# Attention with a learned feature map plus a gated MLP: V weights in halves, and part of the MLP's elementwise work moved from VectorE to ScalarE and GpSimd

## The chip, the cores and the metric

One core of one Trainium2 chip. The metric is the device time of one execution in microseconds (us), as the median of several. Engines: PE is TensorE (matmuls; PEld its weight loads), DVE is VectorE, ACT is ScalarE, POOL is GpSimd, SP issues the DMAs. SBUF and PSUM are the two on-chip memories that this kernel uses; its matmuls write PSUM, which it divides into banks. Most executions of one kernel lie within 0.7% of each other (before: 281.5 to 283.3 us in its first six runs).

## The reference, cut to what matters

2048 tokens of width 640 are normalized. Two branches read the result, and both are added to the input.

```python
def _A_ref(x, wqkv, w_phi, wo):             # 32 heads of 20
    qkv = ...(x @ wqkv)...                  # q, k, v
    pq = einsum("bhsd,hdf->bhsf", q, w_phi) # the same for pk
    phi_q = concat([softmax(pq), softmax(-pq)])   # the same for phi_k
    kv  = einsum("bhsf,bhsd->bhfd", phi_k, v);  z = sum of phi_k over s
    num = phi_q @ kv;  den = phi_q @ z + 1e-6
    return (num / den).reshape(B, S, D) @ wo

def _B_ref(x, w1, w3, w2):                  # F = 1536
    return (silu(x @ w1) * (x @ w3)) @ w2

return x + _A_ref(layernorm(x), ...) + _B_ref(layernorm(x), ...)
```

## The kernel before

The kernel orders its own instructions. The body yields units of work (a K tile, an MLP unit, an attention tile and so on) in eight streams. At each step a greedy scheduler asks a small cost model which unit could start on PE first, and emits that one. The order on every engine is therefore fixed when the kernel is built, from modelled times.

```python
def tt(eng, o, a, b, f, fast=1):            # a two-input elementwise operation
    c = 0.16 + free(o) / 960 / fast if eng == "DVE" else 0.2 + free(o) * 1.7 / 1000
    P.op(eng, "tensor_tensor", [o], [a, b], (o, a, b, f), cost=c)
...
best = None                                 # the scheduler, for each stream's next unit
    at = max(P.ready(ops), P.free["PE"] + 0.15)
    if i == MLPS and P.free["DVE"] > P.free["PE"] + LAG:    # LAG = 4.0
        rank = n                            # an MLP unit comes last while DVE lags
    if best is None or (round(at, 2), rank) < best[:2]: best = ...
```

An MLP unit is 10 matmuls of 512 columns into two PSUM banks, one tanh on ACT, and two DVE instructions.

```python
act(th[:, n, :], bank(k), ACT.Tanh, 0.5)
stt(t1[:, n, :], th[:, n, :], 1.0, bank(k), ALU.add, ALU.mult)
stt(hT[b][:, fc, :], t1[:, n, :], 0.5, bank(k + 1), ALU.mult, ALU.mult)
```

An attention tile (128 tokens) is 12 small matmuls into four PSUM banks. ACT copies the denominators out, DVE combines them, multiplies them into the four banks (`prod`) and adds two halves. `pr`, `den` and `g` are tiny, and **each reads two tensors that lie in SBUF**. The next tile's matmuls reuse the four banks, so they wait for `prod`.

```python
# ... matmuls into four banks, seen as ps[:, n, head, 22]; columns 20 and 21 are denominators
for sg in range(2):
    act(e[:, sg:4 - sg:3 - 2 * sg, :]..., ps[:, 2 * sg:2 * sg + 2, :, 20:22], ACT.Copy)
tt("DVE", pr, e[:, 0:2, :], e[:, 2:4, :], ALU.mult)
tt("DVE", den, pr[:, 0, :], pr[:, 1, :], ALU.add)
P.op("DVE", "reciprocal", [den], [den], (den, den), cost=0.42)
tt("DVE", g, e[:, 2:4, :], den.unsqueeze(1).to_broadcast([128, 2, 32]), ALU.mult)
tt("DVE", p2..., ps[:, :, :, 0:DH], g.unsqueeze(3)..., ALU.mult)        # prod: PSUM x SBUF
tt("DVE", o_tok[:, t % 3, :], p2[:, 0, :], p2[:, 1, :], ALU.add, 2)
```

The start loads the tokens and V's weights, and normalizes four tiles; V and K tiles are projections. Before the first K tile, PE multiplies the feature map's weights into K's weights; this is called the fold here. Up to about 90 us tokens are normalized and V and K tiles are made (the token stage); the attention tiles follow (the attention stage).

```python
load_x(0, 1); load_x(1, 2); load_x(2, 4)
P.dma("SP", wv[:], wqkv_t[:, :, 2 * D:3 * D])
...
for t in range(4):                          # on DVE, in this order
    yield lambda t=t: ln_stats(t, 1)
    if t:
        yield lambda t=t: ln_apply(t - 1)
...
def proj(t, w, k):                          # a V or K tile
    for i in range(DC):
        for q in range(2):
            mm(bank(k + q, 320), xnT[:, i, ...], w[:, i, 320 * q:320 * q + 320], ...)
```

The softmax here doesn't subtract the row's maximum and nothing guards it: scores larger than these inputs give would overflow.

## Time and profile before

| | before |
|---|---|
| median of six runs | 282.28 us |
| profiled span | 280.7 us |
| PE busy | 274.5 us (98%) |
| DVE, ACT, POOL busy | 182.7, 106.9, 59.1 us |
| all matmuls but the last, each at the usual time from start to start of its width | 271.4 us (1889 matmuls, 639,648 columns) |
| first to last matmul start | 276.7 us |

The last two rows are worked out from the starts of the matmuls in the trace. The usual time is the mean of the intervals within 10% of the median: 215.8 ns for 512 columns, 135.8 for 320, 67.0 for 154, 38.4 for 88. The difference of the rows, 5.2 us, is all that PE lost.

The head of the page of before, then rows of its picture of the span in 40 slices. A digit is the busy share of one slice of 7.0 us in tenths.

```profile
PE 274.5 (98%) x1890; PEld 168.4 (60%) x1890; DVE 182.7 (65%) x320; ACT 106.9 (38%) x191; POOL 59.1 (21%) x90
...
PE   7899999999999999999999999999999999999996
...
DVE  5469969999564689989989997886663212121212
...
POOL 4417466999951000000000000000000000000000
```

PE is full (digit 9) from the third slice to the last but one. POOL is busy while K tiles are made (up to slice 12) and **idle in the attention stage**, where DVE is nearly full: from 92 to 190 us POOL is busy 0.43 us and DVE 86.6 of 98. The chain of work that ended last, followed back from the last instruction, by engine:

```profile
PE 94%; DMA 4%; SPq 2%; issue 0%; DVE 0%
```

Groups of instructions of before: engine, operation, output<-inputs, shapes, count | busy us, mean ns of one | idle before it.

```profile
L101 POOL TENSOR_TENSOR ekt<-ekt,rS_62 128x640 bf16<-128x640 bf16 x32 | 39.5, 1271 | 2.3 <-DVE rS_62 L101 2.3
...
L101 DVE TENSOR_TENSOR o_tok<-prod 128x640 bf16<-128x640 bf16 x16 | 7.9, 492 | 0.5
...
L101 DVE TENSOR_TENSOR pr_s<-e_s 128x64 f32<-128x64 f32 x16 | 3.6, 225 | 0.9 <-ACT e_s L101 0.4
L101 DVE TENSOR_TENSOR g_s<-e_s,den_s 128x64 f32<-128x64 f32 x16 | 3.6, 225 | 0.6
...
L101 DVE TENSOR_TENSOR den_s<-pr_s 128x32 f32<-128x32 f32 x16 | 3.1, 191 | 0.6
```

### The profile page before, as it was taken

What the parts mean: (1) busy time and instruction counts of PE and PEld (TensorE: products, weight loads), DVE (VectorE), ACT (ScalarE), POOL (GpSimd) and SP (SyncE); (2) the same over time, 40 slices, a digit from 0 to 9 for tenths busy, and PEclk for the clock granted to TensorE, in tenths of its full rate; (3) what the DMA queues carried; (4) which work ended last, traced back from release to release, by engine and by line L of the source; (5) the groups of instructions that cost most, each with busy time, mean ns of one, the idle gap of its engine ahead of it and who ended that gap; (6) DMA issues with size and microseconds to landing.
All of it is one profiled execution on the core that took longest, in us unless ns stands there. A gap on an engine that the chain in (4) does not pass through costs nothing.

```text
span 280.7 us, 4627 instructions
## 1 busy us (share of the span) xinstructions
PE 274.5 (98%) x1890; PEld 168.4 (60%) x1890; DVE 182.7 (65%) x320; ACT 106.9 (38%) x191; POOL 59.1 (21%) x90
## 2 busy tenths in 40 slices
PE   7899999999999999999999999999999999999996
PEld 2665765775469655555555565744446777777774
DVE  5469969999564689989989997886663212121212
ACT  3379969888520354464464522132221000000000
POOL 4417466999951000000000000000000000000000
PEclk9999999999999999999999999999999999999999
DMA  6973899630000672211111321230000131222211
GB/s 205 282 219 62 235 267 218 92 116 2 0 0 2 206 147 44 29 25 23 26 33 37 26 47 48 60 83 1 2 0 0 50 92 56 86 66 76 71 49 47
DMA packets 39654, 21.96 MB, mean 78 GB/s; under 512 B 26704, under 2 KB 39632, under 8 KB 39632
## 3 DMA queue, kind: packets, MB, share of 16 engines
q1 hardware_dynamic: 39632, 21.66, 32.0%
q8 instruction: 15, 0.25, 0.4%
q14 instruction: 7, 0.06, 0.1%
HBM read 12.81 MB, written 2.62 MB: 55 GB/s over the span
## 4 chain that ended last, share of the span: by engine, by line
PE 94%; DMA 4%; SPq 2%; issue 0%; DVE 0%
PE PS L101 94%; DMA wqkT<-in_A_wqkv_dram 4%; SPq L113 2%; DVE xres L101 0%
## 5 line engine op out<-in xcount | busy, mean ns | idle before, releaser
L101 PE MATMUL PS<-xnT,w_s 128*128 128x512 bf16 x480 | 106.7, 379 | 0.0
L101 PEld LDWEIGHTS PS<-xnT,w_s 128*128 128x128 bf16 x480 | 46.8, 98 | 55.5
L101 ACT ACTIVATE th<-PS 128x512 f32<-128x512 f32 x48 | 28.7, 597 | 57.9 <-PE PS L101 57.9
L101 DVE TENSOR_TENSOR xres<-PS,xres 128x640 bf16<-128x640 f32 (+2 forms) x17 | 13.4, 785 | 54.0 <-PE PS L101 54.0
L101 DVE SCALAR_TENSOR_TENSOR t_68<-th,PS 128x512 bf16<-128x512 f32 x48 | 32.8, 683 | 17.2 <-ACT th L101 17.2
L101 POOL TENSOR_TENSOR ekt<-ekt,rS_62 128x640 bf16<-128x640 bf16 x32 | 39.5, 1271 | 2.3 <-DVE rS_62 L101 2.3
L101 PE MATMUL PS<-wv,xnT 128*128 128x320 bf16 x160 | 24.2, 299 | 0.9 <-DMA wv<-in_A_wqkv_dram 0.9
L101 PE MATMUL PS<-wo_s,oT 128*128 128x320 bf16 (+2 forms) x160 | 24.5, 299 | 0.0
L101 DVE TENSOR_TENSOR prod<-PS,g_s 128x1280 bf16<-128x1280 f32 x16 | 23.9, 1491 | 0.6
L101 PE MATMUL PS<-Wkp,xnT 128*128 128x320 bf16 x160 | 23.9, 299 | 0.1
L101 PE MATMUL PS<-xnT,Wqp 128*128 128x512 bf16 x100 | 23.7, 379 | 0.0
L101 DVE TENSOR_REDUCE S_61<-ekt 128x64 f32<-128x1280 bf16 x16 | 23.0, 1438 | 0.0
L101 ACT ACTIVATE ekt<-PS 128x640 bf16<-128x640 f32 x32 | 20.7, 699 | 5.3 <-PE PS L101 5.0
L101 PEld LDWEIGHTS PS<-wv,xnT 128*128 128x128 bf16 x160 | 15.5, 98 | 6.9 <-ACT xnT L101 1.1
L101 PEld LDWEIGHTS PS<-wo_s,oT 128*128 128x128 bf16 x160 | 15.6, 98 | 6.1
L101 PEld LDWEIGHTS PS<-Wkp,xnT 128*128 128x128 bf16 x160 | 15.3, 98 | 6.3 <-ACT ekt L101 0.2
L101 DVE BATCH_NORM_STATS2 bst<-x_tok 128x6 f32<-128x320 bf16 x32 | 15.2, 476 | 5.4 <-DMA x_tok<-in_A_x_dram 4.9
L101 ACT ACTIVATE e_s<-PS 128x64 f32<-128x64 f32 x32 | 9.0, 282 | 21.9 <-PE PS L101 20.9
L101 PEld LDWEIGHTS PS<-xnT,Wqp 128*128 128x128 bf16 x100 | 9.4, 98 | 8.8
L101 PE MATMUL PS<-w_s,hT_79 128*128 128x320 bf16 (+2 forms) x96 | 13.9, 299 | 0.0
L101 PE MATMUL PS<-w_s,hT_71 128*128 128x320 bf16 x96 | 13.7, 299 | 0.0
L101 PE MATMUL PS<-w_s,hT_76 128*128 128x320 bf16 x96 | 13.7, 299 | 0.0
(59 smaller groups left out, 265.7 us busy)
## 6 DMA issues: line engine op xcount, KB each, us to landing
w_s<-in_B_w_dram SPq DMA_DIRECT2D x6, 640.0 KB, 7.4
xres<-in_A_x_dram SPq DMA_DIRECT2D x16, 160.0 KB, 2.4
out_dram<-xres SPq DMA_DIRECT2D x15, 160.0 KB, 1.8
x_tok<-in_A_x_dram SPq DMA_DIRECT2D x3, 640.0 KB, 5.8
w_s<-in_B_w_dram SPq DMA_DIRECT2D x1, 1920.0 KB, 9.4
wv<-in_A_wqkv_dram SPq DMA_DIRECT2D x1, 800.0 KB, 6.4
wo_s<-in_A_wo_dram SPq DMA_DIRECT2D x1, 800.0 KB, 4.7
x_tok<-in_A_x_dram SPq DMA_DIRECT2D x2, 160.0 KB, 2.3
```

The costliest lines, as they stand in the source:

```text
L101: o = _Op(eng, lambda: m(*args, **kw), r, w, cost)
L113: o = _Op(eng, lambda: m(out, in_), self.regions(in_), self.regions(out), nbytes, True)
```

## The change

Its intent: start V earlier, and take work off DVE, which lags in the attention stage, by giving ACT and POOL a share of it. When the model finds DVE late, ACT copies the second MLP bank from PSUM to SBUF (`up`), and POOL instead of DVE makes the product `hT`. POOL may also add the attention halves. To pay for `up` in SBUF, the tanh buffers go from three to two.

```diff
-        load_x(2, 4)
-        P.dma("SP", wv[:], wqkv_t[:, :, 2 * D:3 * D])
+        load_x(2, 3)
+        for a in (0, 320):
+            P.dma("SP", wv[:, :, a:a + 320], wqkv_t[:, :, 2 * D + a:2 * D + a + 320])
+        load_x(3, 4)
...
     def proj(t, w, k):
-        for i in range(DC):
-            for q in range(2):
+        for q in range(2):
+            for i in range(DC):
...
-        tt("DVE", o_tok[:, t % 3, :], p2[:, 0, :], p2[:, 1, :], ALU.add, 2)
+        eng = "POOL" if P.free["POOL"] < P.free["DVE"] else "DVE"
+        tt(eng, o_tok[:, t % 3, :], p2[:, 0, :], p2[:, 1, :], ALU.add, 2)
...
-        act(th[:, n, :], bank(k), ACT.Tanh, 0.5)
-        stt(t1[:, n, :], th[:, n, :], 1.0, bank(k), ALU.add, ALU.mult)
-        stt(hT[b][:, fc, :], t1[:, n, :], 0.5, bank(k + 1), ALU.mult, ALU.mult)
+        act(th[:, m, :], bank(k), ACT.Tanh, 0.5)
+        half = max(P.free["DVE"], P.free["ACT"] + 0.6, P.free["PE"] + 1.8) + 0.7
+        if max(half, P.free["ACT"] + 1.2, P.free["POOL"]) + 1.1 < half + 0.7 + 0.5 * (P.free["DVE"] - P.free["PE"]):
+            act(up[:, m, :], bank(k + 1), ACT.Copy, 0.5)
+            stt(t1[:, n, :], th[:, m, :], 1.0, bank(k), ALU.add, ALU.mult)
+            tt("POOL", hT[b][:, fc, :], t1[:, n, :], up[:, m, :], ALU.mult)
+        else:
+            ...                            # as before
```

Cut: the declarations of `up` and of two tanh buffers, and the model's DMA rate (320 to 305 thousand bytes per us).

More of the change, by code (lines that the diff above doesn't have):

```diff
@@ L178, in commit @@
                     self.free[o.eng] = t + max(1.3, o.cost / 150e3)
-                self.bus = max(self.bus, t + 0.5) + o.cost / (280e3 if o.part else 320e3)
+                self.bus = max(self.bus, t + 0.5) + o.cost / (280e3 if o.part else 305e3)
                 o.end = self.bus + 1.6
@@ L255, in bass_parallel_sum__linear_kernel_hedgehog__glu_gated_swiglu__prompt_kernel @@
     bf = DT.bfloat16
+    LAG = 4.0
     f32 = DT.float32
@@ L293, in bass_parallel_sum__linear_kernel_hedgehog__glu_gated_swiglu__prompt_kernel @@
     Wqp = new("Wqp", [128, DC, D], bf)
-    th = new("th", [128, 3, 512], f32)
+    th = new("th", [128, 2, 512], f32)
     t1 = new("t1", [128, 3, 512], bf)
+    up = new("up", [128, 2, 512], bf)
     xres = new("xres", [128, 4, D], bf)
@@ L573, in q_tok @@
            g.unsqueeze(3).to_broadcast([128, 4, 16, DH]), ALU.mult)
-        tt("DVE", o_tok[:, t % 3, :], p2[:, 0, :], p2[:, 1, :], ALU.add, 2)
+        eng = "POOL" if P.free["POOL"] < P.free["DVE"] else "DVE"
+        tt(eng, o_tok[:, t % 3, :], p2[:, 0, :], p2[:, 1, :], ALU.add, 2)
     nmlp = [0]
     def mlp(b, fc, k):
-        n = nmlp[0] % 3
+        n, m = nmlp[0] % 3, nmlp[0] % 2
         nmlp[0] += 1
@@ L585, in mlp @@
                    i == 0, i == DC - 1)
-        act(th[:, n, :], bank(k), ACT.Tanh, 0.5)
-        stt(t1[:, n, :], th[:, n, :], 1.0, bank(k), ALU.add, ALU.mult)
-        stt(hT[b][:, fc, :], t1[:, n, :], 0.5, bank(k + 1), ALU.mult, ALU.mult)
+        act(th[:, m, :], bank(k), ACT.Tanh, 0.5)
[5 more added lines that the diff above has]
+        else:
+            stt(t1[:, n, :], th[:, m, :], 1.0, bank(k), ALU.add, ALU.mult)
+            stt(hT[b][:, fc, :], t1[:, n, :], 0.5, bank(k + 1), ALU.mult, ALU.mult)
     finish = []
@@ L757, in outs @@
             yield lambda t=t: out_tile(t, banks(2))
-    MLPS, LAG = 6, 4.0
+    MLPS = 6
     URGENT = {0: 4.0, 3: 4.0}
```

## The prediction

Cuts in the text below are marked. One is a formula for the time of a matmul that is not taken from these traces, with the 271.2 us that it gave for all of them; the 5.4 us that the text goes on with is the 276.7 us less that. (From the trace's own intervals it is 5.2 us, in the table above.) The next is a term of 2.8 us for the first, slow matmuls, where the trace has 1.6 us. "At best about 2.5 us" was the estimate, near 5.4 less 2.8. The forecast's sum came to -0.4 to +0.5 us, centre +0.1, from the four numbered steps.

> **What bounds the kernel now.** TensorE. The page gives PE busy 274.5 us of a 280.7 us span (98%), DVE 65%, ACT 38%, POOL 21%; the chain that ended last is 94% PE and 4% one DMA (the transposing load of the K weights, 5.47 to 15.40 us).[...] first to last start took 276.7. Of the 5.4 us between, 4.8 lie before 16 us (timeline): [...]holes of 0.8 (first transpose), 0.3, 1.1 (V weights, landed 8.63) and 0.8 (K weights, landed 15.40). Later only about 0.7 us is lost, near 17, 47.4 and 48.1 us. At best the change can win about 2.5 us; 2% is 5.7 us.
>
> **What the change does.**
> 1. V weights in halves ahead of tile 3. V's first matmul waited until 8.77 us; the transposes of tiles 0 and 1 were done at 7.83. The first half should land near 6.2 (estimate: 410 KB at the old load's 278 GB/s), so V starts near 7.8: 0.9 gained. But tile 3 lands at 8.6 to 9.1 instead of 5.68, and DVE, in order, runs its statistics (1.0 us) before it normalizes tile 2, whose transpose goes from 10.12 to 10.4-10.7: the 0.9 is given back as a new hole. V ends near 15.4 instead of 14.8, about when the K weights land (15.4 to 15.8[...]). The fold starts at 15.6 to 15.9 instead of 15.54. Net 0 to 0.4 us lost.
> 2. V and K by column half: same matmuls and weight loads, 0 us in steady state. The first K tile needs all five folded chunks by its fifth matmul instead of its ninth (last eviction ended 18.29, K began 17.26): up to 0.5 us of hole, unless an MLP unit is put there, which I expect.
> 3. MLP up over ACT and POOL: DVE loses 0.687 us a unit, ACT gains 0.59, POOL about 1.05 (estimate from 1.271 us for a 640-element product). I guess 10 to 25 of 48 units. No PE wait of size after 17 us ends on DVE: 0 us.
> 4. Attention adds on POOL: DVE loses up to 16 x 0.492 = 7.9 us, POOL gains 16 x about 1.27 = 20. POOL is idle from about 90 us on. Latency grows 0.8 us, with tens of us of output work behind it: 0 us.
>
> Sum: -0.4 to +0.5 us, centre +0.1. PE has the same columns to pass and was not starved in the middle.
>
> **Predicted:** 282.9 us, 8 in 10 between 281.2 and 284.5 (the runs before spread 1.8 us). Faster by over 2%: 0.01; within 2%: 0.96; slower: 0.03.
>
> **What would show it.** Right: PE busy within 1 us of 274.5; DVE busy down 12 to 25 us, POOL up 30 to 45, span nearly unmoved; first V matmul near 7.8, then a wait of 0.5 to 1.3 us for normalized tile 2; fold at 15.5 to 16. Wrong: fold or first K over 0.5 us earlier, or PE holes over 0.3 us after 20 us.
>
> **What would make it wrong.** The static order comes from modelled times, so every engine's order can shift; a POOL product slowed by DVE beside it, or two tanh buffers instead of three, could hold PSUM banks and stall PE in the token stage. Or the MLP order fills the early holes: up to 1.5 us won.

## More of the kernel before

The model knows one duration for each instruction and the waits between instructions. It knows nothing of two engines hindering each other.

(The trace has 1.6 us for the first, slow matmuls: eight intervals of 0.39 to 0.43 us for 512 columns, at a granted clock of 1.00. Why they are slow is not shown.)

One attention tile in the timeline of before: start us, duration us, engine and so on. Lines of ACT, PEld and the DMA are left out.

```profile
118.20 0.85 PE L101 MATMUL PS<-KVc,EqT_81 128*128 128x154 bf16 x12
...
119.40 0.23 DVE L101 TENSOR_TENSOR pr_s<-e_s 128x64 f32<-128x64 f32 x1
119.66 0.19 DVE L101 TENSOR_TENSOR den_s<-pr_s 128x32 f32<-128x32 f32 x1
...
120.27 0.23 DVE L101 TENSOR_TENSOR g_s<-e_s,den_s 128x64 f32<-128x64 f32 x1
120.53 1.49 DVE L101 TENSOR_TENSOR prod<-PS,g_s 128x1280 bf16<-128x1280 f32 x1
```

From the first small matmul to the end of `prod` takes 3.8 us. The next tile's matmuls may then begin, but PE has other work meanwhile: in this order two MLP units (4.3 us) and a Q projection stand between most attention tiles.

## The result, and the profile after

The changed kernel takes 293.15 us (median of six, 292.17 to 293.65) against 282.28 us. The ratio is 1.038, with a 95% interval of 1.035 to 1.041. Ratios here and below are the mean time of one kernel's fast runs over that of the other's of the same rounds, so not quite the ratio of the medians. The prediction, 282.9 us with a range to 284.5, was wrong by 10 us.

The head of the page of the changed kernel, and the same rows of its slices (7.3 us each):

```profile
PE 275.9 (95%) x1872; PEld 167.4 (58%) x1890; DVE 175.2 (60%) x289; ACT 123.0 (42%) x221; POOL 98.3 (34%) x124
...
PE   7899989999999997988988999999999999999996
...
DVE  5378879996554699999999996445432121121212
...
POOL 4416868999932222222222534322310000000000
```

PE does the same work in 95% of a longer span: slices 16 to 22 now have gaps. POOL is busy in the attention stage. DVE gave up 31 instructions (320 to 289) yet saved only 7.5 us of busy time. (18 of the 1890 matmul records are missing from this trace.) The chain that ended last:

```profile
PE 73%; DVE 18%; DMA 3%; ACT 2%; SPq 2%; issue 1%
PE PS L101 73%; DVE prod L101 7%; DVE pr_s L101 5%; DVE den_s L101 3%; DMA wqkT<-in_A_wqkv_dram 3%; SPq L113 2%; DVE t_68 L101 1%; ACT e_s L101 1%; DVE g_s L101 1%; ACT up L101 1%; DVE o_tok L101 1%; ACT v_83 L101 0%; DVE xres L101 0%
```

DVE went from 0% to 18% of that chain, by way of the attention tile's own operations. The groups that answer to those of before, and POOL's new work:

```profile
L101 DVE TENSOR_TENSOR pr_s<-e_s 128x64 f32<-128x64 f32 x16 | 16.0, 1002 | 2.8 <-ACT e_s L101 1.4
...
L101 POOL TENSOR_TENSOR hT_78<-t_68,up 128x512 bf16<-128x512 bf16 x12 | 13.8, 1152 | 40.5 <-DVE t_68 L101 29.5 <-ACT e_s L101 11.0
...
L101 DVE TENSOR_TENSOR den_s<-pr_s 128x32 f32<-128x32 f32 x16 | 5.6, 352 | 0.6
L101 DVE TENSOR_TENSOR g_s<-e_s,den_s 128x64 f32<-128x64 f32 x16 | 3.6, 225 | 0.6
...
L101 POOL TENSOR_TENSOR o_tok<-prod 128x640 bf16<-128x640 bf16 x1 | 1.4, 1392 | 5.1 <-DVE prod L101 5.1
```

`pr_s`, the same 64 elements per partition, takes 1002 ns instead of 225, and `den_s` 352 instead of 191. Together that is 16.0 + 5.6 - 3.6 - 3.1 = 14.9 us more. `g_s` is unchanged. One tile in the timeline shows why:

```profile
128.96 0.86 PE L101 MATMUL PS<-KVc,EqT_82 128*128 128x154 bf16 x12 [0.73 <-DVE prod L101]
...
130.10 1.15 POOL L101 TENSOR_TENSOR hT_78<-t_68,up 128x512 bf16<-128x512 bf16 x1 [3.68 <-DVE t_68 L101]
130.17 1.16 DVE L101 TENSOR_TENSOR pr_s<-e_s 128x64 f32<-128x64 f32 x1
...
131.37 0.19 DVE L101 TENSOR_TENSOR den_s<-pr_s 128x32 f32<-128x32 f32 x1
...
131.98 0.23 DVE L101 TENSOR_TENSOR g_s<-e_s,den_s 128x64 f32<-128x64 f32 x1
...
132.24 1.49 DVE L101 TENSOR_TENSOR prod<-PS,g_s 128x1280 bf16<-128x1280 f32 x1
...
133.79 0.86 PE L101 MATMUL PS<-KVc,EqT_76 128*128 128x154 bf16 x12 [0.73 <-DVE prod L101]
```

POOL's product runs from 130.10 to 131.25. `pr_s` starts at 130.17 and ends at 131.33, just behind it. The same sight recurs: of the 48 executions of `pr_s`, `den_s` and `g_s`, 18 are long. Each of these 18 has a POOL product beside it and ends 0.05 to 0.08 us after that product. The 30 others take their usual time.

The loop closes over PSUM. From one tile's small matmuls to the next is 133.79 - 128.96 = 4.83 us. PE has only 3.93 us of work in it (0.69 for the 12 attention matmuls, 1.08 for a Q projection, 2.16 for an MLP unit, all at the usual times from start to start), so it waits 0.90 us for `prod`. (The timeline prints 0.73 us of idle time, because the modelled end of the matmul before it reaches into the gap.) Such holes between 103 and 175 us sum to 9.5 us, nearly the whole 9.7 us by which the profiled span grew. (In that sum gaps of 0.216 us are left out: they are the missing matmul records, all of 512 columns. The trace of the path alone, below, has all 1890 and shows the same holes, 9.5 us from 100 us on.)

The start behaved in part as predicted. V began at 7.67 instead of 8.77 us, and PE then lost 0.80 us at 8.9 us to normalized tile 2. The first half of V's weights landed at 6.30 us (predicted 6.2) and the second at 7.70. But tile 3 landed at 8.17 us, where I had predicted 8.6 to 9.1, and the fold began at 15.12 instead of the predicted 15.6 to 15.9. Differences of this size are not safe to read from one trace: V's weights in one piece (800 KB), with the very same loads before them in the queue, landed anywhere from 7.50 to 9.01 us in six traces (before, b1, b3, b4, c1 and e1; in order of size 7.50, 8.12, 8.17, 8.43, 8.63 and 9.01), and V began between 7.92 and 9.14 us.

### The profile page after: what moved, and what is told of

Same layout as the page of the kernel before. It is cut to its first block, busy times and chain, and to the rows that moved or that the text cites. A ratio compares the mean times of both kernels' runs of the same rounds, so it can differ in the third digit from the quotient of the medians.

```text
span 290.5 us, 4679 instructions
## 1 busy us (share of the span) xinstructions
PE 275.9 (95%) x1872; PEld 167.4 (58%) x1890; DVE 175.2 (60%) x289; ACT 123.0 (42%) x221; POOL 98.3 (34%) x124
## 4 chain that ended last, share of the span: by engine, by line
PE 73%; DVE 18%; DMA 3%; ACT 2%; SPq 2%; issue 1%
PE PS L101 73%; DVE prod L101 7%; DVE pr_s L101 5%; DVE den_s L101 3%; DMA wqkT<-in_A_wqkv_dram 3%; SPq L113 2%; DVE t_68 L101 1%; ACT e_s L101 1%; DVE g_s L101 1%; ACT up L101 1%; DVE o_tok L101 1%; ACT v_83 L101 0%; DVE xres L101 0%
## 5 line engine op out<-in xcount | busy, mean ns | idle before, releaser
L101 POOL TENSOR_TENSOR hT_78<-t_68,up 128x512 bf16<-128x512 bf16 x12 | 13.8, 1152 | 40.5 <-DVE t_68 L101 29.5
L101 ACT ACTIVATE up<-PS 128x512 bf16<-128x512 f32 x33 | 19.7, 598 | 15.4 <-PE PS L101 15.4
L101 DVE TENSOR_TENSOR prod<-PS,g_s 128x1280 bf16<-128x1280 f32 x16 | 23.9, 1491 | 0.5
L101 PE MATMUL PS<-xnT,Wqp 128*128 128x512 bf16 x93 | 22.2, 379 | 0.4
L101 PEld LDWEIGHTS PS<-Wkp,xnT 128*128 128x128 bf16 x160 | 15.4, 98 | 7.2 <-ACT ekt L101 1.1
L101 DVE TENSOR_TENSOR pr_s<-e_s 128x64 f32<-128x64 f32 x16 | 16.0, 1002 | 2.8 <-ACT e_s L101 1.4
L101 POOL TENSOR_TENSOR hT_72<-t_68,up 128x512 bf16<-128x512 bf16 x9 | 10.2, 1152 | 16.3 <-DVE t_68 L101 10.3
```

Source lines behind the costliest of these rows:

```text
L101: o = _Op(eng, lambda: m(*args, **kw), r, w, cost)
```

## The experiments

Theory S: a DVE operation with two SBUF inputs is held until the POOL instruction beside it ends. Theory O: the new order alone starves PE, because one MLP unit instead of two stands between attention tiles. Theory A: ACT's extra copies and the two tanh buffers hold PSUM banks.

| run | edit | median us | before, same rounds | ratio (95%) |
|---|---|---|---|---|
| a1_one_sbuf_input | after, `pr`, `den`, `g` with one SBUF input | 283.66 | 282.62 | 1.004 (1.000 to 1.008) |
| a2_no_mlp_path | after without the MLP path (two tanh buffers and the choice of engine for the add stay) | 294.63 | 282.62 | 1.043 (1.038 to 1.047) |
| b1_mlp_path_only | before with the MLP path | 292.79 | 282.62 | 1.037 (1.033 to 1.042) |
| b2_start_only | before with the early part | 291.32 | 282.62 | 1.031 (1.026 to 1.036) |
| b3_pool_two_input | before + unused POOL products | 293.00 | 281.88 | 1.037 (1.030 to 1.043) |
| b4_pool_one_input | before + unused POOL copies | 289.21 | 281.88 | 1.023 (1.017 to 1.029) |
| b5_start_lag5 | b2 with the lag limit 5 us | 285.51 | 281.88 | 1.010 (1.004 to 1.016) |
| c1_path_one_sbuf | b1 with a1's edit | 282.87 | 281.88 | 1.001 (0.996 to 1.007) |
| e1_fold_later | before, an MLP unit ahead of the fold | 282.49 | 282.40 | 1.002 (0.999 to 1.005) |
| e6_order_only | e1, V weights ahead of tile 3 | 283.46 | 282.40 | 1.004 (1.001 to 1.007) |
| e7_path_order | e6 + MLP path + a1's edit | 283.51 | 282.40 | 1.005 (1.001 to 1.008) |
| e2_all_fixed | after, all three mended | 282.97 | 282.40 | 1.003 (1.000 to 1.005) |

All outputs are right. Three or five rounds were run of each, so a run has four or six executions, and those of "before" are of the same rounds. b4's interval reaches from below to above 1.02, but all of it lies well above 1.

### The same order, without the second SBUF input

```diff
-        tt("DVE", pr, e[:, 0:2, :], e[:, 2:4, :], ALU.mult)
-        tt("DVE", den, pr[:, 0, :], pr[:, 1, :], ALU.add)
-        P.op("DVE", "reciprocal", [den], [den], (den, den), cost=0.42)
-        tt("DVE", g, e[:, 2:4, :], den.unsqueeze(1).to_broadcast([128, 2, 32]), ALU.mult)
+        tt("DVE", pr..., ps[:, :, :, 20], e[:, 2:4, :]..., ALU.mult)        # PSUM x SBUF
+        P.op("DVE", "tensor_reduce", [den], [pv], (den, pv, AX.X, ALU.add), ...)  # one input
+        dps = PS[:, k * 512 + 352:k * 512 + 384]       # unused columns of the tile's own bank
+        o = P.op("DVE", "reciprocal", [dps], [den], (dps, den), cost=0.42)
+        P.op("DVE", "tensor_tensor", [g], ..., (g, e[:, 2:4, :], db, ALU.mult), ...)  # db: dps; SBUF x PSUM
```

The kernel's own bookkeeping does not see a DVE write to PSUM that DVE reads next. An explicit dependency mended it. Modelled costs were kept, and the built program has the same order of instructions as the changed kernel on PE, ACT, POOL and DVE; only these operations differ. The POOL products, the ACT copies and the two tanh buffers all stay.

> The changed kernel with an unchanged order of instructions on all engines; only DVE's small attention ops (pr_s, den_s, g_s) no longer read two SBUF tensors: each reads one SBUF and one PSUM tensor, or one tensor. Theory S (a DVE op with two SBUF inputs is held until the POOL product beside it ends): pr_s falls from 1.00 us mean to under 0.3, the PE holes between 100 and 175 us go, and the time falls from about 293 to 283-286 us. Theory O (the new order alone, with an MLP unit between nearly all attention tiles, starves PE) and theory A (the added ACT copies and only two tanh buffers hold PSUM banks): 291-294 us.

Measured: 283.66 us, 9.5 us below the changed kernel (1.004 of before in its rounds, against 1.038). Two groups, and a tile of its timeline:

```profile
L102 DVE TENSOR_TENSOR pr_s<-PS,e_s 128x64 f32<-128x64 f32 x16 | 3.6, 224 | 5.6 <-ACT e_s L102 4.3
...
L102 POOL TENSOR_TENSOR hT<-t,up 128x512 bf16<-128x512 bf16 x33 | 37.9, 1153 | 73.2 <-ACT up L102 36.6 <-DVE t L102 36.6
```

```profile
122.41 1.15 POOL L102 TENSOR_TENSOR hT<-t,up 128x512 bf16<-128x512 bf16 x1 [2.97 <-DVE t L102]
122.48 0.23 DVE L102 TENSOR_TENSOR pr_s<-PS,e_s 128x64 f32<-128x64 f32 x1
122.74 0.22 DVE L102 TENSOR_REDUCE den_s<-pr_s 128x32 f32<-128x64 f32 x1
```

The same POOL product of 1.15 us runs beside `pr_s`, which now takes 0.23 us. In the stretch from 93 to 176 us PE is busy 83.0 of 83.0 us, against 75.5 in the changed kernel (76.1 in b1 below, whose trace lacks no matmul record). It is the second SBUF input that counts, and not SBUF as such: `den_s`, now a reduction of one SBUF tensor, lay beside a POOL product in 15 of its 16 executions and took 0.22 us in all of them. Theories O and A fall: with their order, copies and buffers in place the loss is gone. Consecutive attention tiles with one MLP unit between them now follow each other in 3.93 us (`pr_s` at 118.55 and 122.48 us), exactly PE's own work.

### A POOL instruction added to the kernel before

```diff
         stt(hT[b][:, fc, :], t1[:, n, :], 0.5, bank(k + 1), ALU.mult, ALU.mult)
+        if done["kv"]:                     # 39 of the 48 units; nobody reads `spare`
+            a = t1[:, n, 0:448].unsqueeze(1).to_broadcast([128, 2, 448])
+            P.op("POOL", "tensor_tensor", [o], [t1[:, n, :]], (o, a, a, ALU.mult), cost=0.01)
```

`o` is a view of `spare`, which takes unused bytes. The second run has two `tensor_copy` of the same 896 elements instead of the product. In both the order on PE, ACT and DVE is that of before.

> The kernel before with its order of instructions unchanged on PE, ACT and DVE; after each MLP unit of the attention stage POOL multiplies an 896-element bf16 tile with itself into a scratch tile that nobody reads (about 1.9 us, an estimate from 1.152 us for 512). Nothing else is changed, so nothing of order, tanh buffers or ACT copies. Theory S: pr_s beside it is held, to 1 us or more in most of 16 tiles, PE waits for prod, and the time rises by 4 to 14 us. Any theory that needs the new order or the ACT copies: 282 to 283.5 us and pr_s at 0.23.

> As the run before, but POOL makes two copies of 896 elements (one input each) instead of one product. If every POOL instruction holds DVE's ops with two SBUF inputs: pr_s near 1 us again and 4 to 14 us lost. If only POOL's two-input products hold them: pr_s at 0.23 us and 282 to 283.5 us.

Measured: 293.00 and 289.21 us. The groups of the run with products, then those of the run with copies:

```profile
L101 DVE TENSOR_TENSOR pr_s<-e_s 128x64 f32<-128x64 f32 x16 | 22.2, 1386 | 0.1
...
L101 POOL TENSOR_TENSOR spare<-t 128x896 bf16<-128x896 bf16 x39 | 65.6, 1681 | 67.4 <-DVE t L101 65.2
```

```profile
L101 DVE TENSOR_TENSOR den_s<-pr_s 128x32 f32<-128x32 f32 x16 | 12.9, 804 | 0.5
...
L101 DVE TENSOR_TENSOR g_s<-e_s,den_s 128x64 f32<-128x64 f32 x16 | 7.4, 461 | 0.6
...
L101 POOL COPY spare<-t 128x896 bf16<-128x896 bf16 x78 | 72.6, 931 | 56.4 <-DVE t L101 50.9
```

So POOL work that nobody needs, with no new order, no ACT copies and three tanh buffers, costs 11 us as products and 7 us as copies. The longer instruction holds longer: `pr_s` beside a 1.68 us product takes up to 1.71 us. A one-input copy of 0.93 us holds as well. There `pr_s` mostly slips in between two copies (263 ns in the mean) and `den_s` and `g_s` are caught instead. My alternative, that only products hold, is wrong. (`prod`, which reads PSUM and SBUF, took 1491 ns in every run, but in no trace did it run beside a POOL instruction, so it tests nothing. What does is `t`, which also reads PSUM and SBUF: in the changed kernel 14 of its 48 executions began inside a POOL product, and took 0.69 us, where the others took 0.63 to 0.69.)

### One part of the change at a time

> The kernel before with the ACT and POOL path of the MLP alone. All theories that blame the path: 291 to 294 us, with pr_s near 1 us. Under 286 would say that the path hurts only together with the other parts.

Measured: 292.79 us, with `pr_s` at 1.0 us again. The path alone carries the loss. With a1's edit on top (c1):

> The kernel before with the ACT and POOL path of the MLP and DVE's one-SBUF-input attention ops, without the early part. Theory S: 282 to 284 us, 8 to 11 us below the path alone (292.8).

Measured: 282.87 us and a ratio of 1.001 instead of 1.037, as expected.

> The changed kernel without the ACT and POOL path of the MLP (all 48 units as before); V halves, half-by-half order, two tanh buffers and the choice of engine for the attention add stay. Theories S, O and A all say 281.5 to 283.5 us, as before. If the early loads or the halves carry part of the loss: 284 us or more.

> The kernel before with the early part alone: V weights in halves ahead of tile 3, V and K by column half, the scheduler's DMA rate. From the trace of the changed kernel (fold starts at 15.1 instead of 15.54 us): 281 to 282.5 us, so 0 to 1 us better than before. My first sum (0 to 0.4 us lost) would say 282.5 to 283.

Both missed badly: 294.63 and 291.32 us. The early part by itself (b2) also makes the kernel slow, but not in the same way. `pr_s` took 225 ns there. The changed kernel shows nothing like the following stretch of b2's timeline on PE:

```profile
171.61 1.60 PE L101 MATMUL PS<-KVc,EqT 128*128 128x154 bf16 x24
175.49 1.08 PE L101 MATMUL PS<-KVc,EqT 128*128 128x154 bf16 x12 [2.28 <-DVE prod L101]
178.56 2.85 PE L101 MATMUL PS<-wo_s,oT 128*128 128x320 bf16 x10 [1.99 <-DVE prod L101]
```

Changed early costs made the greedy scheduler choose another order 170 us later. With T for an attention tile, M for an MLP unit and O for output work, the end of the stage is `MMTOTMMTOTMMM` in before, but `MMTOTTTOMMM` here. Three tiles in a row leave PE with nothing to do while `prod` runs. Behind the holes the 320-column matmuls start 267 ns apart instead of 136 for about 4 us, and the page's granted clock falls to 6 and 8 tenths in two slices of 7.2 us. Half the clock is what this trace shows, from 176.0 to 182.8 us, behind a hole of 2.4 us. The granted clock of the whole execution, 0.988, fits that: half the clock for 6.9 of its 289.3 us (an estimate). What makes the clock fall is not shown. I tested the order with one constant:

```diff
-    MLPS, LAG = 6, 4.0
+    MLPS, LAG = 6, 5.0
```

> The early part alone once more, with the scheduler's lag limit 5 us instead of 4. In the run of the early part alone the scheduler had put three attention tiles in a row (no MLP unit between), with PE holes of 2.4 and 2.3 us[...]; with 5 us no two attention tiles stand side by side. If that order was the loss and not the loads: 281.5 to 283.5 us and a granted clock of 1.00. If the loads or the halves cost: 288 us or more.

Measured: 285.51 us and a granted clock of 1.00. The 2 us holes and the low clock are gone, and with them 5.8 us. It still missed my range. Its profiled span is 2.2 us over that of before: PE lost 0.8 us at 37.5, 0.6 us more near 46 and 0.9 us between 180 and 187 us. Its median is 3.6 us over; the trace is of its fastest execution (284.67 us), and it does not show the rest. In a2 the same thing happened as in b2, with four tiles in a row and holes of 2.5, 3.0 and 1.8 us. But a2 was not free of the hold either: there the scheduler moved 14 of the 16 attention adds to POOL, and `den_s` was held behind such an add twice, for 1.35 us. Once was this:

```profile
163.14 1.39 POOL L101 TENSOR_TENSOR o_tok<-prod 128x640 bf16<-128x640 bf16 x1 [4.66 <-DVE prod L101]
163.22 1.35 DVE L101 TENSOR_TENSOR den_s<-pr_s 128x32 f32<-128x32 f32 x1
```

The `prod` behind it ended the 3.0 us hole, so some 1.2 us of that hole is the hold (an estimate: 1.35 less the usual 0.19). So these two runs say nothing of the loads or halves as such. They show that "one part alone" is not a clean experiment when a scheduler re-plans everything behind it.

### Is there a version that beats both?

With the hold away, only the early holes are left to win. These runs had five rounds.

```diff
     def fold_k():
+        while nmlp[0] < 1:                 # e1, e2, e6, e7: one MLP unit first
+            yield None
...
-            yield lambda t=t: ln_stats(t, 1)     # e2, e6, e7: tile 3's statistics
+            if t < 3: ...                        # after tile 2 is normalized
```

> The kernel before, with one MLP unit put between the fourth V tile and the fold of the K weights, which in the trace of before waits 0.8 us for its weights. If PE's holes alone set the time, 0.5 to 0.9 us less than before: a ratio of about 0.997. The 2% line is out of reach.

> As the run before, and V's weights (in one piece) loaded ahead of token tile 3, with tile 2 normalized before tile 3's statistics, so that the hole the changed kernel has at 8.9 us does not arise. V should start near 7.8 instead of 8.8 us: 1.3 to 2 us less than the kernel before, a ratio of about 0.994.

> The run before plus the ACT and POOL path of the MLP with DVE's one-SBUF-input attention ops. DVE then has slack in the attention stage, PE had no hole there anyway: the same time as the run before within 0.5 us. If the path is worth something by itself, it shows here and nowhere else.

> The whole change with its three weak places mended: one-SBUF-input attention ops, tile 2 normalized before tile 3's statistics, an MLP unit ahead of the fold. 280.5 to 282.5 us, against 283.7 with the first alone.

None of them gains: ratios of 1.002, 1.004, 1.005 and 1.003. In e1 the 0.8 us hole before the fold did go, but PE then waited 0.6 us at 39 us and 0.7 at 47 us, where before had 0 and 0.2. The line at 39 us names what it waited for:

```profile
39.51 1.25 PE L101 MATMUL PS<-Wkp,xnT 128*128 128x320 bf16 x8 [0.45 <-DMA xnT<-x_tok]
```

That is the next normalized, transposed token tile. PE had come earlier to a point that it does not set. In e6, V's weights in one piece landed at 8.55 us, and in e7, with the same loads before them, at 8.91 us, although the fourth token tile had been taken out from in front of them; my 7.8 us for V's start was wrong. In e2, in two pieces, they were complete at 7.63 us, and e2 won 1.1 us before 10 us and gave it back at 39 and 47 us (0.7 and 0.8 us, where before had 0 and 0.2). Each of these orders closed early holes and opened others near 39 and 47 us, and a landing that varies by 1.5 us from run to run is as large as what they were after. That no order can win is not shown.

## Why the prediction was wrong

The step that failed is number 3: "No PE wait of size after 17 us ends on DVE: 0 us." The arithmetic treated each engine's load by itself: DVE minus 0.687 us a unit, POOL plus 1.05. The missing term is what a POOL instruction does to the DVE instruction beside it: 14.9 us of longer `pr_s` and `den_s` in 16 tiles. PE then waited 9.5 us for `prod`. That the wait did not exist before was taken to mean that it could not arise. Before, POOL worked only in the token stage, and DVE's two-SBUF operations on the PSUM loop ran only in the attention stage. The change put both in the same place.

All held instructions end 0.04 to 0.09 us after POOL's, whether POOL's takes 0.93, 1.15 or 1.68 us. So most of a held operation's own 0.19 to 0.23 us was not paid again. (Here it was always DVE that came second; POOL being held by DVE was not seen.) In a1 the DVE operations with at most one SBUF input were not held: 0.22 to 0.23 us beside a product of 1.15 us. The traces show the hold and its length, not what in the hardware causes it. The prediction took POOL's rate from the trace of before (1.271 us for a 640-element product) and did not ask what DVE would do beside it.

Point by point:

- TensorE bounds the kernel, and "at best the change can win about 2.5 us": not contradicted. No version beat before.
- Early part, "0 to 0.4 us lost": the 0.80 us hole for tile 2 came as said (0.5 to 1.3). The K weights did not land later (14.98 us, against 15.40 before and 15.4 to 15.8 predicted), and the fold came 0.4 us earlier than before. Both sizes were off by less than 1 us, which is within the spread of the landings.
- Half order, "an MLP unit is put there": right, one stands ahead of the first K tile.
- MLP path, "10 to 25 units": 33. "About 1.05" us on POOL: 1.152. "0 us": 9.5 us. This is the error.
- Attention adds, up to 16 on POOL: the scheduler moved one. In a2 it moved 14, and there two of them held `den_s`, at some 1.2 us in a PE hole. So "0 us" was wrong there for the same reason.
- DVE "down 12 to 25 us": down 7.5, because the held time counts as busy. POOL "up 30 to 45": up 39.2.
- The warning named "a POOL product slowed by DVE beside it". It is the other way round: POOL's product kept its 1.152 us and DVE waited. The check "PE holes over 0.3 us after 20 us" did catch it.

Left open: how much the hold costs at before's own spacing of two MLP units with products of 1.15 us (b3 used longer ones), and whether two half loads of V's weights land earlier than one: with tile 3 behind them they were complete at 7.63 to 8.32 us in six traces, one load at 8.55 and 8.91 us in two, and both lie within what the one load in its old place had (7.50 to 9.01 us).

## What to carry to other kernels

Before moving work to an idle engine, ask what runs beside it then. Here POOL's products (1.15 and 1.68 us) and copies (0.93 us), which read SBUF, held DVE's operations with two SBUF inputs until they ended, and a 0.2 us operation on a PSUM loop then cost 1 us. (Shown for three float32 operations of 32 or 64 elements; the bf16 add `o_tok` never ran on DVE beside POOL.) If the two must overlap, let the short DVE operations read one operand from PSUM, or use a one-input form; here that took back 9.5 us without changing the order. The rates alone (a 640-element bf16 add took 1.392 us on POOL and 0.492 on DVE) leave this out: 33 products of 1.152 us on POOL also cost DVE 14.9 us. When a scheduler re-plans the kernel, compare builds with an identical order, because a part taken alone can lose as much for a reason of its own.
